# Two of four gate-logit rows summed on VectorE, w_gate turned in the prologue, and g split at the end of its own step

## The chip, the cores and the metric

The kernel runs on one core of one Trainium2 chip. Its time is the device time of one execution in microseconds (us). Of the kernel before there are three timed runs, told by their median, and one profiled execution. PE is TensorE, DVE is VectorE, ACT is ScalarE, POOL is GpSimd, and SP is SyncE, which here only issues transfers.

## The reference

Three parts follow one another: attention between 4096 tokens and 256 state rows (8 batches, 8 heads of 64), a layer g(h) = h - tanh(h) between two matrices, and a mixture of 8 experts that takes the best expert of each of 4608 rows.

```python
xread = softmax(scale * x @ state.T) @ state      # per batch and head
sread = softmax(scale * state @ x.T) @ x
x = concat(xread, sread).reshape(4608, 512)
h = x @ w_in                                      # 512 -> 2048
y = (h - tanh(h)) @ w_out                         # 2048 -> 512
logits = y @ w_gate                               # 512 -> 8
e = argmax(logits)
gate = softmax(logits)[e]
out[row] = gate * (relu(y @ w1[e]) @ w2[e])       # 512 -> 1024 -> 512
```

## The kernel before

The large products are taken in three parts: each operand is split into a high part that is exact in the fast matmul format and a low rest, and hi*hi, hi*lo and lo*hi are added up in PSUM. w_in and w_out come as 64-bit numbers, and three DVE operations (L186, L188, L191) with one of ACT turn a piece of 128 x 512 into float32: its decoding, `dec_bits`.

The work has three stages, one after the other:

- The prologue (up to about 130 us) does the attention scores, and multiplies the state with w_in, so that later h comes straight from the attention's probabilities. Its loop loads x in units (`xc`), three of them ahead; a list `later` holds stores, which SP issues at the head of each turn (`flush`, L451).
- The group stage (to about 779 us) runs 9 groups of rows. Groups 0 to 7 hold the 512 tokens of a batch as 4 rows of 128 each ("row" here is one such block of 128 tokens), group 8 holds the 256 state rows. Each group has 16 steps, one for each 128 of the 2048 columns of h. Step i does on PE `mm1(i)` (L828, six matmuls into `hp`), then `mm2(i-2)` (L858, twelve matmuls, three for each of the 4 rows, that add to the PSUM tiles y0 to y3). Between them lies the polynomial for g: ACT squares hp twice (L207, L208), DVE multiplies twice (L210, L211) into `gs`, `g_split` writes the high part `gh` (ACT, L847) and the rest `gl` (DVE, L160), and `g_check` (ACT, L840) records whether hp left the range of the polynomial. `hp` has two PSUM buffers, `gs` two, `gh` and `gl` three.
- The expert stage (to the end) takes blocks of 128 rows of one expert each. The change doesn't touch it.

In the group stage the order on PE, ACT, DVE and SP is that of the code, and each engine works in order. Four lists (`between`, `beside`, `after`, `moves`) say what else goes into which step, and where in it: `between` after mm1 on PE, `beside` after `g_split`, `after` behind `g_check`, `moves` last (transfers). While group 0 runs, w_out is decoded and split in every step; in groups 1 to 7 w_in is decoded again for group 8 in two or three steps of each (0 and 8, in groups 1 and 2 also 4), and a step later POOL takes the rest of that split. The operands of mm1 are split in steps 1, 2, 5, 6, 9, 10, 13 and 14 (`swl`), and in 10 and 12 (`atl`).

When a group is done, its rows are finished beside the next group's steps. In step 1, y0 to y3 are copied to `ys` in SBUF (three by ACT, one by DVE). Then each row r goes, two steps apart, through five operations: PE turns it with four transposes (`turn`, L263, end of step 2 + 2r), DVE copies the result (`turned`, L271, step 3 + 2r), PE multiplies it with w_gate in `parts` (L277, eight instructions, step 5 + 2r), ACT copies the partial sums (L283), and PE adds them up in `total` (L286, two instructions, step 6 + 2r). In step 12, when all four rows have their logits, DVE picks the expert (`choose`); `count` and `place` find each token's place in that expert's list.

## Time and profile before

| | |
|---|---|
| median of 3 runs | 1282.85 us (1280.61 to 1283.53) |
| profiled execution | 1281.19 us, span of its trace 1279.5 us |
| PE busy | 1229.9 us (96%) |
| DVE busy | 885.7 us (69%) |
| ACT busy | 858.0 us (67%) |
| POOL busy | 249.7 us (20%) |
| PE's share of the chain that ended last | 83% (L858 28%, L1426 16%, L1453 15%, L828 14%) |

Busy time counts an instruction from its start to its end; neighbours on one engine overlap, so what an instruction costs in a row of its kind is read from the starts, not from its length: twelve matmuls that each last 0.4 us start 0.23 us apart. A wait is the idle time before an instruction, put down to what ended it. The chain of waits goes back from the last instruction to what released each one.

### The profile page before, as it was taken

The numbers are of one execution on the slowest core, as the hardware profiler recorded it, in microseconds if no ns is written. First come the engines' busy times: TensorE is split into PE (matmuls) and PEld (weight loads), VectorE is DVE, ScalarE is ACT, GpSimd is POOL, SyncE is SP. The second block draws the span as 40 slices with busy tenths as digits, with TensorE's granted clock in tenths as the row PEclk, the third lists the DMA queues.
The fourth block names the chain that finished last, engine by engine and source line by source line (L and its number), as shares of the span: only waits on it lengthen the run. The fifth ranks groups of instructions, "written<-read, shape, count | busy, mean of one in ns | idle before, by whom it ended". The sixth has DMA issues, their size and how long they took to land.

```text
span 1279.5 us, 22682 instructions
## 1 busy us (share of the span) xinstructions
PE 1229.9 (96%) x6759; PEld 974.8 (76%) x6759; DVE 885.7 (69%) x1531; ACT 858.0 (67%) x1587; POOL 249.7 (20%) x299
## 2 busy tenths in 40 slices
PE   6989798999999999999999999999999999999995
PEld 4555576777777878778787888788888888888884
DVE  6999899677666766576666557567667677675663
ACT  7988687667676767667676674566666657565562
POOL 3333222011010101001010122322223322221100
PEclk8999899999999999999999999999999999999998
DMA  7999652413232222312222471744587867744241
GB/s 259 330 317 292 217 146 81 148 59 124 83 99 71 77 73 61 112 57 96 83 95 66 122 270 43 247 173 157 202 315 268 303 238 283 262 144 182 95 161 68
DMA packets 85777, 207.23 MB, mean 162 GB/s; under 512 B 9794, under 2 KB 26181, under 8 KB 83858
## 3 DMA queue, kind: packets, MB, share of 16 engines
q1 hardware_dynamic: 71186, 161.28, 37.8%
q0 software_dynamic: 14464, 44.40, 9.8%
q8 instruction: 62, 1.02, 0.3%
q14 instruction: 65, 0.53, 0.2%
HBM read 314.90 MB, written 74.51 MB: 304 GB/s over the span
## 4 chain that ended last, share of the span: by engine, by line
PE 83%; DVE 8%; DMA 4%; ACT 2%; issue 1%; SPq 0%; POOL 0%; DVEq 0%; POOLq 0%; ACTq 0%
PE y L858 28%; PE h L1426 16%; PE o L1453 15%; PE hp L828 14%; PE pt_h L1441 2%; DMA xc<-in_x_dram 2%; PE px L1264 1%; PE pt_y L263 1%; DVE dec_m L188 1%; DVE dec_m L191 1%; DMA atf<-probs_t 1%; DMA words<-in_moe_w_out_dram 1%; PE lg L277 1%; PE h_lead L1024 1%; DVE gl L160 1%
## 5 line engine op out<-in xcount | busy, mean ns | idle before, releaser
L858 PE MATMUL y<-w1t,gh 128*128 128x512 f32 x544 | 223.6, 411 | 2.2 <-ACT gh L847 2.2
L858 PE MATMUL y<-w1t,gl 128*128 128x512 f32 x544 | 218.3, 401 | 7.7 <-DVE gl L160 7.7
L210 DVE SCALAR_TENSOR_TENSOR gs<-gs,gu 128x512 f32<-128x512 f32 (+1 forms) x144 | 95.3, 662 | 179.2 <-ACT gs L208 167.6
L858 PE MATMUL y<-w,gh 128*128 128x512 f32 x544 | 215.7, 397 | 0.0
L1453 PE MATMUL o<-w2t,w 128*128 (+1 forms) x888 | 212.5, 395 | 0.8 <-DVE w2t L1370 0.8
L1426 PE MATMUL h<-w1t,w 128*128 (+1 forms) x888 | 212.2, 394 | 0.0
L1370 DVE TENSOR_TENSOR w2t<-w2raw,w2t 128x1024 f32 (+1 forms) x140 | 171.3, 1226 | 39.0 <-ACT w2t L1369 30.0
L1453 PEld LDWEIGHTS o<-w2t,w 128*128 128x128 f32 x888 | 163.9, 188 | 34.8 <-issue 1.2
L1426 PEld LDWEIGHTS h<-w1t,w 128*128 128x128 f32 x888 | 163.9, 188 | 33.7 <-issue 0.4
L207 ACT ACTIVATE gu<-hp 128x512 f32<-128x512 f32 (+1 forms) x144 | 82.4, 573 | 158.2 <-PE hp L828 157.8
L1369 ACT CAST w2t<-w2raw 128x1024 f32 (+1 forms) x140 | 147.1, 1053 | 17.0 <-DMA w2raw<-in_moe_w_dram 6.6
L858 PEld LDWEIGHTS y<-w1t,gl 128*128 128x128 f32 x544 | 103.3, 190 | 38.2 <-DVE gl L160 13.8
L828 PE MATMUL hp<-ath,swh 128*128 128x512 f32 (+1 forms) x320 | 122.5, 383 | 4.5 <-ACT ath L367 2.9
L858 PEld LDWEIGHTS y<-w1t,gh 128*128 128x128 f32 x544 | 103.0, 189 | 29.7 <-issue 6.4
L828 PE MATMUL hp<-atl,swh 128*128 128x512 f32 (+1 forms) x320 | 119.5, 373 | 0.9 <-DVE atl L368 0.9
L858 PEld LDWEIGHTS y<-w,gh 128*128 128x128 f32 x544 | 103.6, 190 | 21.8
L828 PE MATMUL hp<-ath,swl 128*128 128x512 f32 (+1 forms) x320 | 118.5, 370 | 0.0
L1432 ACT ACTIVATE hs<-h 128x512 f32<-128x512 f32 x74 | 43.8, 598 | 107.0 <-PE h L1426 102.8
L208 ACT ACTIVATE gs<-gu,b 128x512 f32<-128x512 f32 (+1 forms) x144 | 101.0, 701 | 7.1 <-DVE gl L160 1.9
L840 ACT ACTIVATE gu<-gu,nlim 128x512 f32<-128x512 f32 (+1 forms) x144 | 100.4, 697 | 6.4 <-DVE gs L210 5.0
L211 DVE SCALAR_TENSOR_TENSOR gs<-gs,hp 128x512 f32<-128x512 f32 (+1 forms) x144 | 94.6, 657 | 4.9
L160 DVE TENSOR_TENSOR gl<-gs,gh 128x512 fp32r<-128x512 f32 (+1 forms) x133 | 97.4, 733 | 0.0
(257 smaller groups left out, 1849.5 us busy)
## 6 DMA issues: line engine op xcount, KB each, us to landing
w1t<-w_parts SPq DMA_DIRECT2D x35, 4096.0 KB
w2raw<-in_moe_w_dram SPq DMA_DIRECT2D x140, 512.0 KB
w_parts<-w POOLq DMA_DIRECT2D x48, 512.0 KB
mot<-in_moe_w_dram SPq DMA_DIRECT2D x72, 256.0 KB
state_w_in<-swst SPq DMA_DIRECT2D x32, 512.0 KB
swf<-state_w_in SPq DMA_DIRECT2D x64, 256.0 KB
words<-in_moe_w_in_dram SPq DMA_DIRECT2D x16, 512.0 KB
xc<-in_x_dram SPq DMA_DIRECT2D x16, 512.0 KB
```

The source lines that it names most:

```text
L160: return eng.tensor_tensor(lo, t, hi.bitcast(F32), op=ALU.subtract)
L207: nc.scalar.activation(u, hp, AF.Square)
L208: nc.scalar.activation(s1, u, AF.Square, bias=b1)
L210: nc.vector.scalar_tensor_tensor(s1, s1, QD, u, op0=ALU.add, op1=ALU.mult)
L211: nc.vector.scalar_tensor_tensor(s1, s1, QC2, hp, op0=ALU.mult, op1=ALU.mult)
L828: nc.tensor.matmul(hp, a[:, c, o : o + P], m[:, c, :], start=(n == 0), stop=(n == 3 * chunks - 1))
L840: nc.scalar.activation(u, u, AF.Relu, bias=nlim, accum_out=over[:, n : n + 1])
L858: mm = nc.tensor.matmul(y, g, w[f], start=(f == 0 and n == 0), stop=(f == NF - 1 and n == 2))
L1369: hi = nc.scalar.copy(to[0](i * CH), t)
L1370: lo = nc.vector.tensor_tensor(to[1](SLOT + i * CH), t, to[1](i * CH).bitcast(F32), op=ALU.subtract)
L1426: mm = nc.tensor.matmul(h, a[:, k, :], part(w1t, o1, lo_ * SLOT + k * F2 + half * NX), start=(n == 0), stop=(n == 11),)
L1453: mm = nc.tensor.matmul(o, a[:, k, :], part(w2t, o2, lo_ * SLOT + k * DM), start=(n == 0), stop=(n == 23))
```

## The change

There are three parts.

- **Sums on DVE.** For groups 0 to 6, rows 0 and 1 no longer go through `turn`, `turned`, `parts`, copy and `total`. For each of these rows and each of the 8 experts DVE multiplies the row of 512 with that expert's column of w_gate, laid out along the free dimension and repeated on all partitions (`wgb`), and adds up the product in the same instruction (`sums`, one scalar_tensor_tensor with `accum_out`; the product itself goes to `junk`). That is 16 instructions of 128 x 512 per group, put into steps 2 to 11: two each in steps 2, 3, 5, 7, 8 and 10, one in 4, 6, 9 and 11. Rows 2 and 3 keep their path and their steps. `choose` first copies their logits from PSUM next to the sums. Group 7 and group 8 stay as they were.
- **w_gate turned.** In the prologue PE turns w_gate (four transposes of 128 x 32, `turn_gate`, behind the first `attn_x`), DVE copies the result of 8 x 512, and SP stores it to DRAM at the next `flush`. In steps 2 to 9 SP loads each of its 8 rows back onto all 128 partitions, 256 KB each. `wgb` lies in a half of `w1t` that held four of the eight `pairs`, the ring through which the w_in parts go; the ring now has four. PSUM for the logits is taken when it is first used, no longer when a group's finish begins.
- **g_split.** `gh` and `gl` of step i were made in step i + 1, right behind the two multiplications for that step. They are now made at the end of step i, behind `beside` and `g_check` (in step 0 ahead of `beside`).

```diff
--- before.py
+++ after.py
@@ -1,3 +1,4 @@
+import functools
 import itertools
 from contextlib import ExitStack
 
@@ -42,6 +43,7 @@
         "w1": nc.dram_tensor("w1_parts", (E * P, 2, DM // P * F2), F32).ap(),
         "wi": nc.dram_tensor("w_in_parts", (FF // (2 * P), P, 2, 2, DM), F32).ap(),
         "at": nc.dram_tensor("probs_t", (B, P, 2, S), F32).ap(),
+        "wg": nc.dram_tensor("w_gate_t", (E, DM), F32).ap(),
         "sw": nc.dram_tensor("state_w_in", (FF // NX, B // 4, H, 4, NS, NX), F32).ap(),
     }
     args = (tc, x, state, w_in.bitcast(I32), w_out.bitcast(I32), w_gate, w1, w2, out, scratch)
@@ -83,8 +85,8 @@
 
     NSURE = NBLK + (E - 1) * 3 // 4
     scale = 1.0 / float(D) ** 0.5
-    yd, lists, w1s, wis, atd, swd = (
-        scratch[k] for k in ("y", "list", "w1", "wi", "at", "sw")
+    yd, lists, w1s, wis, atd, swd, wgd = (
+        scratch[k] for k in ("y", "list", "w1", "wi", "at", "sw", "wg")
     )
 
     const = ctx.enter_context(tc.tile_pool(name="const", bufs=1))
@@ -228,13 +230,26 @@
             self.pool, self.psp, self.b = pool, psp, b
             self.nr = R if b < B else NSR
             self.pt, self.yT = {}, {}
-            lg = psp.tile([P, 3 * R * E + P], F32, tag="lg", name="lg")
-            self.lg = lg[:, 0 : 3 * self.nr * E].rearrange("p (i r e) -> p i r e", i=3, e=E)
-            self.lgt = lg[:, 3 * R * E :]
             self.ys = pool.tile([P, self.nr, DM], F32, tag="ys", name="ys", bufs=1)
+
+            self.summed = 0 if b > B - 2 else self.nr // 2
+            if self.summed:
+                self.logit = pool.tile([P, self.nr, E], F32, tag="logit", name="logit", bufs=2)
             self.lgs = pool.tile([P, self.nr, E], F32, tag="lgs", name="lgs", bufs=2)
             self.entry = pool.tile([P, self.nr, 2], F32, tag="entry", name="entry", bufs=2)
             nc.gpsimd.tensor_copy(self.entry[:, :, 0], ridf[:, b * R : b * R + self.nr])
+
+        @functools.cached_property
+        def bank(self):
+            return self.psp.tile([P, 3 * R * E + P], F32, tag="lg", name="lg")
+
+        @property
+        def lg(self):
+            return self.bank[:, 0 : 3 * self.nr * E].rearrange("p (i r e) -> p i r e", i=3, e=E)
+
+        @property
+        def lgt(self):
+            return self.bank[:, 3 * R * E :]
 
         def take(self, r, y):
             if r < self.nr - 1:
@@ -285,6 +300,13 @@
         def total(self, r):
             nc.tensor.matmul(self.lg[:, 0, r], self.lgs2, sel, start=True, stop=True)
 
+        def sums(self, r, e):
+            junk = self.pool.tile([P, DM], F32, tag="junk", name="junk", bufs=1)
+            nc.vector.scalar_tensor_tensor(
+                junk, self.ys[:, r], 1.0, wgb[:, e], op0=ALU.mult, op1=ALU.mult,
+                accum_out=self.logit[:, r, e : e + 1],
+            )
+
         def logits(self, r):
             yT = self.yT.pop(r)
             for k in range(NPR):
@@ -297,7 +319,9 @@
 
         def choose(self):
             nr, lgs = self.nr, self.lgs
-            lg = self.lg[:, 0]
+            lg = self.logit if self.summed else self.lg[:, 0]
+            if 0 < self.summed < nr:
+                nc.vector.tensor_copy(lg[:, self.summed :], self.lg[:, 0, self.summed :])
             mx = self.small("rmx")
             nc.vector.tensor_reduce(mx, lg, axis=AX.X, op=ALU.max)
             mxb = mx.unsqueeze(2).to_broadcast([P, nr, E])
@@ -491,6 +515,14 @@
             c = slice(2 * k, 2 * k + 2)
             nc.scalar.copy(sth[:, c], st[:, c])
             rest(nc.vector, stl[:, c], st[:, c], sth[:, c])
+
+        def turn_gate():
+            pt = ps_m.tile([P, NPR, P], F32, tag="m", name="pt_gate")
+            for k in range(NPR):
+                nc.tensor.transpose(pt[0:QR, k, :], wg[:, k], ident)
+            t = tmp("e2", (P, NX))
+            nc.vector.tensor_copy(t[0:E], pt[0:E].rearrange("p k m -> p (k m)"))
+            later.append((wgd, t[0:E]))
 
         win = {}
         wdec = Decoder(pa, 3)
@@ -687,6 +719,7 @@
             for o, j in ((0, 0), (0, 4), (1, 0), (1, 4), (1, 8)):
                 turn_state(o, j)
             attn_x(0)
+            turn_gate()
             for i in piece(1):
                 wdec.absolute(i)
                 wdec.bits(i)
@@ -790,6 +823,9 @@
         ps_m = pe.enter_context(tc.tile_pool(name="ps_m", bufs=1, space=PSUM, reuse_waits="tile"))
 
         pairs = w1t[:, 0].rearrange("p h n -> p (h n)").rearrange("p (i h n) -> p i h n", h=2, n=NX)
+        pairs = pairs[:, 0 : pairs.shape[1] // 2]
+
+        wgb = w1t[:, 0, 1, 0 : E * DM].bitcast(F32).rearrange("p (e d) -> p e d", e=E)
         turns = itertools.count()
 
         def pair():
@@ -898,6 +934,12 @@
             put(moves, i + 1, store_win, f)
         for g in range(NF // 2):
             put(moves, B * NF + 2 * g - 3, load_win, g)
+
+        def gate_load(e):
+            nc.sync.dma_start(wgb[:, e], wgd[e : e + 1].to_broadcast([P, DM]))
+
+        for e in range(E):
+            put(moves, 2 + e, gate_load, e)
         def finish(b, i):
             fn = Finish(fin, ps_m, b)
             for r in range(fn.nr):
@@ -905,7 +947,10 @@
             if b == B:
                 return fn
             put(moves, i + 1, fn.store)
-            for r in range(fn.nr):
+            all_ = [(r, e) for r in range(fn.summed) for e in range(E)]
+            for n, a in enumerate(all_):
+                put(beside, i + 1 + n * 10 // len(all_), fn.sums, *a)
+            for n, r in enumerate(range(fn.summed, fn.nr)):
                 j = i + 2 * r
                 put(after, j + 1, fn.turn, r)
                 put(beside, j + 2, fn.turned, r)
@@ -1085,11 +1130,13 @@
                     mm2(b, f)
                     if f == NF - 1:
                         fn = finish(b, i)
-                if 1 <= i <= N:
-                    g_split(*seq[i - 1])
+                if i == 0:
+                    g_split(*seq[i])
                 run(beside, i)
                 if i < N:
                     g_check(*seq[i])
+                if 0 < i < N:
+                    g_split(*seq[i])
                 run(after, i)
                 run(moves, i)
 
```

DVE in steps 7 and 8 of group 1, from the two multiplications of step 7 on; `gs_3238` and `gs_3278` are gs of these steps. Before:

```order
L210 SCALAR_TENSOR_TENSOR gs_3238<-gs_3238,gu 128x512
L211 SCALAR_TENSOR_TENSOR gs_3238<-gs_3238,hp 128x512
L160 TENSOR_TENSOR gl<-gs_3192,gh 128x512
L271 COPY yT<-pt_y 128x512
L210 SCALAR_TENSOR_TENSOR gs_3278<-gs_3278,gu 128x512
L211 SCALAR_TENSOR_TENSOR gs_3278<-gs_3278,hp 128x512
L160 TENSOR_TENSOR gl<-gs_3238,gh 128x512
L186 TENSOR_SCALAR dec_l<-words 128x512
L188 SCALAR_TENSOR_TENSOR dec_m<-dec_m,dec_l 128x512
L191 SCALAR_TENSOR_TENSOR dec_m<-words,dec_m 128x512
```

And now, where the two gs are `gs_3249` and `gs_3290`:

```order
L212 SCALAR_TENSOR_TENSOR gs_3249<-gs_3249,gu 128x512
L213 SCALAR_TENSOR_TENSOR gs_3249<-gs_3249,hp 128x512
L305 SCALAR_TENSOR_TENSOR junk,logit<-ys,w1t 128x512 x2
L286 COPY yT<-pt_y 128x512
L162 TENSOR_TENSOR gl<-gs_3249,gh 128x512
L212 SCALAR_TENSOR_TENSOR gs_3290<-gs_3290,gu 128x512
L213 SCALAR_TENSOR_TENSOR gs_3290<-gs_3290,hp 128x512
L188 TENSOR_SCALAR dec_l<-words 128x512
L190 SCALAR_TENSOR_TENSOR dec_m<-dec_m,dec_l 128x512
L193 SCALAR_TENSOR_TENSOR dec_m<-words,dec_m 128x512
L305 SCALAR_TENSOR_TENSOR junk,logit<-ys,w1t 128x512 x2
L162 TENSOR_TENSOR gl<-gs_3290,gh 128x512
```

The gl that stands behind the two multiplications of a step was that of the step before; now each step ends with its own, behind the decoding and the two sums.

ACT in steps 2 and 3 of group 1, where `gs_2977` was the g of step 1 and `gs_3023` that of step 2. Before:

```order
L207 ACTIVATE gu<-hp 128x512
L208 ACTIVATE gs_3023<-gu,b_70 128x512
L847 CAST gh<-gs_2977 128x512
L367 CAST swh<-swf 128x512
L840 ACTIVATE gu,over<-gu,nlim 128x512
L207 ACTIVATE gu<-hp 128x512
L208 ACTIVATE gs_3070<-gu,b_70 128x512
L847 CAST gh<-gs_3023 128x512
L840 ACTIVATE gu,over<-gu,nlim 128x512
```

And now, where `gs_3043` and `gs_3089` are the g of steps 2 and 3:

```order
L209 ACTIVATE gu<-hp 128x512
L210 ACTIVATE gs_3043<-gu,b_70 128x512
L391 CAST swh<-swf 128x512
L876 ACTIVATE gu,over<-gu,nlim 128x512
L883 CAST gh<-gs_3043 128x512
L209 ACTIVATE gu<-hp 128x512
L210 ACTIVATE gs_3089<-gu,b_70 128x512
L876 ACTIVATE gu,over<-gu,nlim 128x512
L883 CAST gh<-gs_3089 128x512
```

gh moves from behind the two squares, where its gs had been done for most of a step, to the end of the step, where the same step's gs has just been made.

SP at the start of the program, from the first piece of w_in on (`words`). Before:

```order
L175 DMA words<-in_moe_w_in_dram 128x1024
L537 DMA xc<-in_x_dram 128x4x256
L175 DMA words<-in_moe_w_in_dram 128x1024
L537 DMA xc<-in_x_dram 128x4x256
L175 DMA words<-in_moe_w_in_dram 128x1024
L537 DMA xc<-in_x_dram 128x4x256
L175 DMA words<-in_moe_w_in_dram 128x1024
L751 DMA expert_lists<-unlisted 128x560
```

And now:

```order
L177 DMA words<-in_moe_w_in_dram 128x1024
L569 DMA xc<-in_x_dram 128x4x256
L177 DMA words<-in_moe_w_in_dram 128x1024
L569 DMA xc<-in_x_dram 128x4x256
L177 DMA words<-in_moe_w_in_dram 128x1024
L477 DMA w_gate_t<-e_246 8x512
L569 DMA xc<-in_x_dram 128x4x256
L177 DMA words<-in_moe_w_in_dram 128x1024
L784 DMA expert_lists<-unlisted 128x560
```

The third load of x, which followed the third piece of w_in at once, now stands behind the store of the turned w_gate.

## Rows read from the trace of the kernel before

**Rows 1.** Windows: span, busy us by engine (instructions), TensorE clock, DMA share, GB/s.

```profile
145.00:200.00 55.00, 50.23 (x194) 37.52 (x194) 52.74 (x74) 44.52 (x87) 15.88 (x12) 0.95 0.52 152
555.00:628.00 73.00, 73.00 (x358) 57.80 (x358) 48.24 (x90) 51.26 (x103) 7.09 (x7) 1.00 0.25 80
```

**Rows 2.** Timeline, PE, groups 5 and 6, mm1's first matmul: start us, us, operation.

```profile
553.48 0.40 PE L828 MATMUL hp<-ath,swh 128*128 128x512 f32 x1
...
558.23 0.40 PE L828 MATMUL hp<-ath,swh 128*128 128x512 f32 x1
...
562.65 0.40 PE L828 MATMUL hp<-ath,swh 128*128 128x512 f32 x1
...
566.84 0.40 PE L828 MATMUL hp<-ath,swh 128*128 128x512 f32 x1
...
584.05 0.40 PE L828 MATMUL hp<-ath,swh 128*128 128x512 f32 x1
...
588.60 0.48 PE L828 MATMUL hp<-ath,swh 128*128 128x512 f32 x1
...
592.88 0.39 PE L828 MATMUL hp<-ath,swh 128*128 128x512 f32 x1
```

**Rows 3.** Timeline, two steps of group 1, PE and DVE (in brackets: idle before).

```profile
240.21 0.40 PE L828 MATMUL hp<-ath,swh 128*128 128x512 f32 x1
...
242.29 0.40 PE L858 MATMUL y<-w1t,gl 128*128 128x512 f32 x1
...
243.19 0.69 DVE L210 SCALAR_TENSOR_TENSOR gs<-gs,gu 128x512 f32<-128x512 f32 x1 [0.44 <-ACT gs L208]
...
243.92 0.69 DVE L211 SCALAR_TENSOR_TENSOR gs<-gs,hp 128x512 f32<-128x512 f32 x1
...
244.52 0.68 DVE L160 TENSOR_TENSOR gl<-gs,gh 128x512 fp32r<-128x512 f32 x1
```

**Rows 4.** Timeline, one step of group 0, DVE and POOL.

```profile
176.47 0.68 DVE L210 SCALAR_TENSOR_TENSOR gs<-gs,gu 128x512 f32<-128x512 f32 x1
...
177.19 0.69 DVE L211 SCALAR_TENSOR_TENSOR gs<-gs,hp 128x512 f32<-128x512 f32 x1
...
177.29 1.30 POOL L160 TENSOR_TENSOR w<-dec_m,w1t 128x512 fp32r<-128x512 f32 x1 [3.14 <-ACT w1t L197]
...
177.79 1.34 DVE L160 TENSOR_TENSOR gl<-gs,gh 128x512 fp32r<-128x512 f32 x1
...
179.06 0.41 DVE L186 TENSOR_SCALAR dec_l<-words 128x512 int32<-128x512 int32 x1
...
180.91 0.68 DVE L210 SCALAR_TENSOR_TENSOR gs<-gs,gu 128x512 f32<-128x512 f32 x1
```

**Rows 5.** Timeline, PE, two of its waits (in brackets: length, releaser).

```profile
195.20 0.63 PE L858 MATMUL y<-w1t,gl 128*128 128x512 f32 x1 [2.28 <-DVE gl L160]
...
776.72 0.50 PE L858 MATMUL y<-w1t,gl 128*128 128x512 f32 x1 [0.63 <-DVE gl L160]
```

**Rows 6.** Groups by line: count | busy us, mean ns | idle before.

```profile
L840 ACT ACTIVATION_READ_ACCUMULATOR gu<-gu,nlim 128x1 f32 x144 | 27.1, 188 | 0.0
...
L271 DVE COPY yT<-pt_y 128x512 f32<-128x512 f32 x29 | 19.7, 681 | 0.3 <-PE pt_y L263 0.3
```

**Rows 7.** Timeline, the prologue's first steps, SP's queue, PE and DVE.

```profile
4.80 0.62 SPq L537 DMA_DIRECT2D xc<-in_x_dram  x1
...
9.41 1.06 PE L548 MATMUL pt_x<-ident,xc 128*128 128x128 f32 x8 [1.25 <-DMA xc<-in_x_dram]
...
11.76 0.69 DVE L188 SCALAR_TENSOR_TENSOR dec_m<-dec_m,dec_l 128x512 int32<-128x512 int32 x1 [1.55 <-ACT dec_m L181]
...
18.52 0.66 PE L548 MATMUL pt_x<-ident,xc 128*128 128x128 f32 x4
```

**Rows 8.** Chain of waits, two of its pieces: start us, us, what.

```profile
44.61 6.27 DMA xc<-in_x_dram
...
172.17 11.50 DMA words<-in_moe_w_out_dram
```

## The prediction, made before the changed kernel ran

> **What bounds the kernel now.** I read first the windows, to see which engine is full in which stretch, then the timeline of PE, step by step, and last who waits for whom. In groups 1 to 7 PE is full: 73.00 of 73 us, while DVE is busy 48.24 and no other engine is near full [rows 1]. There every PE instruction taken out shortens the step by its issue time, as long as no other engine becomes late. Group 0 is different: in its window PE is busy 50.23 of 55 us and DVE 52.74 [rows 1], because the decoding of w_out stands in every step. DVE's operations follow each other without a gap: from one first multiplication to the next 4.44 us [rows 4], where a plain step of PE takes 4.19 (562.65 to 566.84) [rows 2]. So in group 0 work taken from PE would be worth nothing, and the order on DVE decides. No PE instruction is removed there anyway.
>
> **The sums: what PE loses.** The price of one row's path comes from the starts of mm1. A plain step is 4.19 us. The step with `parts` (553.48 to 558.23) is 4.75, so parts cost 0.56. The step with `total` (558.23 to 562.65) is 4.42: 0.23. The step that ends with a row's transposes (584.05 to 588.60) is 4.55: 0.36, and the next (588.60 to 592.88) is 4.28, 0.09 more for the change back to long matmuls [rows 2]. One row costs 0.56 + 0.23 + 0.36 + 0.09 = 1.24 us of PE. Two rows in each of seven groups: 14 x 1.24 = 17.4 us. All of it lies in steps where PE is the bound. This is the main term, -17.4.
>
> **The sums: what DVE gets.** Sixteen instructions per group that read two SBUF tensors of 128 x 512. No row shows one with an accumulator on DVE. Nearest are its multiplications of the same shape: start to start 0.73 us where the second needs the first (243.19 to 243.92) and 0.60 where it doesn't (243.92 to 244.52) [rows 3]. ACT's accumulator shows a second instruction of 188 ns behind each of its own [rows 6]. So a sum costs at least 0.60, and at most two passes of 0.69 and such a read-out, 1.57. I take 0.8, near the multiplication, since nothing in a row shows a two-SBUF multiplication of DVE at half rate.
>
> Does it fit? In steps 2 to 11 DVE has, without the sums, 10 x (0.73 + 0.60 + 0.60) = 19.3 for g, six splits (3.6) and two copies of turned rows (1.2) at 0.60, one decoding at 1.85 (179.06 to 180.91) and one collision with POOL at 0.67 (gl takes 1.27, 177.79 to 179.06, in place of 0.60) [rows 3, 4]: 26.6 us. PE needs for these ten steps 41.9 and for what rows 2 and 3 still bring (two turns 0.90, two parts 1.12, one total 0.23) 2.25, so 44.15. That leaves 17.5 us for 16 sums, or 1.09 each, before DVE falls behind. At 0.8 they take 12.8.
>
> A single step can still be late. With the change gl(i) is the last operation of step i. Its first multiplication starts 2.98 us behind the start of mm1(i) (240.21 to 243.19) and the two and gl itself take 0.73 + 0.60 + 0.68, so gl(i) is there at 5.0 + W, W being what `beside` has on DVE. PE needs it in mm2(i), two steps on: 8.38 + 1.85 = 10.2 us behind mm1(i) (242.29 less 240.21, less the 0.23 of the total in that step) [rows 2, 3]. The slack is 5.2 - W. The fullest step is 8, decoding and two sums, W = 3.45; behind it, steps 9 and 10 start with about 1 us of arrears and W of 2.7 to 2.8. So PE's gl comes in time by 1 to 2 us, and hp too, whose buffer is freed already by the second multiplication. Queued behind the sums on DVE are gl and the next step's multiplications; behind gh on ACT, the next step's squares. In step 1 ACT also copies three y tiles, which makes the squares of step 2 late as before. I put down +1 us for waits in all seven groups (0 to +5). The small copy in `choose` lies in step 12, which has no sums: nothing.
>
> A rule of the Trainium skill speaks against this price: the page "Vector Engine (DVE) Microarchitecture Reference", section "Points that are easy to get wrong", says that a scalar_tensor_tensor with two non-bf16 sources in SBUF runs at half throughput, since both read ports are taken and none is left for the accumulator. The trace has the two-source fp32 multiplication without an accumulator at 0.69 us, not double, and shows none with one. By that rule the sum would come out as in the third rival below.
>
> **g_split at the end of its own step.** In groups 1 to 7 PE hardly waits for gl, so nothing is to be had there. In group 0 gl(i) moves ahead of the next step's two multiplications, of 0.73 and 0.60, and of a collision of 0.67: PE can run mm2(i) up to 2.0 us earlier, and its wait of 2.28 us for gl [rows 5] is of this kind. That lead is kept when DVE stops being the bound, at the start of group 1. I take -2 (0 to -4). DVE's own work doesn't change. What is new is that gh, and so ACT's next squares, hang on the same step's second multiplication; from there gh and two squares take about 2 us on ACT, while DVE has the decoding and gl to do, 1.85 + 0.60, so DVE doesn't idle. POOL's subtraction now starts earlier against DVE's order and will block another operation. A blocked operation waits until POOL's 1.30 us are over [rows 4]: between 0.67, as now, and 1.3 per step. I take +0.5 for the group (0 to +10, 16 steps at 0.63 more). At the end of the stage the wait of 0.63 us in mm2's last step [rows 5] goes: -0.6 (0 to -0.6), and what is late next there is the copy of y.
>
> **w_gate in the prologue.** PE's four transposes stand behind the first x unit, which starts at 9.41 and lasts 1.06; DVE's copy of their result costs 0.68, like the copy of a turned row [rows 6, 7]. So it runs from about 10.95 to 11.6, and the first decoding behind it starts at about 12.1 and not at 11.76. DVE's work is the chain of most of the prologue: +0.4 (0 to +1). SP's third x load was issued at 4.80; now it waits behind the store for that copy, until about 12.1. A load of x took 6.27 us when the DMA engines were full [rows 8], so it would land by 18.4, and PE's transposes of that unit began at 18.52 [rows 7]. It just fits; if not, it costs tenths, which the bound of +1 holds.
>
> The eight loads of `wgb` bring 2 MB into group 0's steps 2 to 9. SP issues them behind the same step's load of w_out. One such load there took 11.50 us and was on the chain [rows 8], while the DMA share was 0.52 [rows 1], so there is room but a piece can be late: +1 (0 to +4).
>
> **Sum.** -17.4 + 1 - 2 + 0.5 - 0.6 + 0.4 + 1 = -17.1. I round to -17. The profiled execution took 1281.19 us, 1.69 outside its span of 1279.5; less 17 that is 1264.2. The median of the runs is 1.66 above the profiled one, so I expect a median of 1266.
>
> **Rivals.** (a) Group 0 gets longer: POOL's collisions cost the full 1.3 in every step (+10), and the w_out loads slip. For it: DVE is full there, and ACT now hangs on it. Against it: the second multiplication ran its 0.69 us beside POOL [rows 4], so one operation per step is blocked, as before. Time: 1266 + 10 = 1276.
>
> (b) Group 0 gets shorter than I say. DVE's step there is 4.44 with a blocked gl of 1.27 in it; were POOL's subtraction, which now starts earlier against DVE's order, to fall beside the decoding, 0.67 would go and DVE would need 3.77, so that PE's 4.19 is the step [rows 2, 4]: 16 x 0.25 = 4, and with POOL's +0.5 gone 4.5. For it: a decoding of 1.85 is long enough to hold 1.30. Against it: it has the same order in each step now, and gl is still the two-SBUF operation behind it. Time: 1266 - 5 = 1261.
>
> (c) A sum costs two passes, 1.38 us. Sixteen take 22.1 where 17.5 fit; 4.6 behind, less the slack of step 11, 5.2 - 1.38 = 3.8: 0.8 us wait per group, and 2.5 more in groups 1 and 2, whose third decoding (1.85 + 0.67) lies in these steps. 7 x 0.8 + 5 = 10.6 lost: 1266 + 10.6 - 1 (the waits counted already) = 1276.
>
> (d) The other side: two passes and a read-out, 1.57 us, make DVE the bound in steps 2 to 11 of groups 1 to 7. Sixteen take 25.1, 7.6 too much; less 3.6 of slack PE waits 4.0 us per group, and with the third decodings 28 + 5 = 33, against 17.4 saved: 1283 + 33 - 17 - 1 = 1298. At s us a sum PE waits 17 x s - 22.7 + 0.7 per group (16 sums, less 17.5 and the slack of 5.2 - s; the third decodings add 5 over seven groups). That passes 0 at 1.3 us, where the gain begins to shrink, and the 2.48 saved per group at 1.44, from where the kernel is slower. For it: no row shows the operation. Against it: all DVE multiplications of this shape last 0.69.
>
> **How the numbers follow.** My forecast 0.60, (a) 0.12, (b) 0.11, (c) 0.08, (d) 0.09. The forecast's own range is 1262 to 1271, from the bounds of its terms taken half. To leave out no more than 2 in 10 I go on to (b) below and to (a) and (c) above: 1260 to 1277. What this kernel's measurement can tell from no change is about 0.2%, 2.6 us. Faster are the forecast, (a), (b) and (c), whose times are all more than 6 us below, less 0.03 for a sum between (c) and (d): 0.88. Slower is (d): 0.09. Within 0.2%: 0.03.
>
> **What would show it.** Right: mm1 starts 4.19 us apart in steps 3, 4 and 5 of groups 1 to 7, where step 3 was 4.28; a group takes 2.48 us less; PE full there; a sum of 0.6 to 0.9 us; DVE busy about 60 of 70 us per group (48.24 less two copies, 16 sums more); PE's waits for gl in group 0 shorter; mm1(0) not more than 1 us later. Wrong: waits of PE for gl or of mm1 for the second multiplication in steps 8 to 12 (the sums are dearer, or the arrears larger); a group 0 longer by several us, with more than one long DVE operation per step or with DVE waiting for `words`; sums of 1.2 us or more.

## The result and the profile after

The changed kernel takes 1260.27 us (median of 4 runs, 1258.44 to 1263.43) against 1281.73 for the kernel before in the same comparison: a ratio of 0.9836, 95% interval 0.9818 to 0.9854, or 21 us less. The forecast was 1266 in a range of 1260 to 1277. The two profiled executions differ by less than the medians: 1281.19 and 1263.43 us, spans 1279.5 and 1261.7, so 17.8 us of span; the profiled execution of the changed kernel is the slowest of its four.

Where the 17.8 us went is read from the first matmul of mm1 in each group's step 0, and from the ends of the spans (us). In group 0 alone the mark is the fourth of mm1's six matmuls, since PE takes the first three ahead of the prologue's last product (`px`), at 130.41 us before and 132.40 after; "group 0" below always counts from that fourth one, and so does "step 0 starts".

| stretch | before | after | difference |
|---|---|---|---|
| prologue, up to the fourth matmul of step 0 | 133.74 | 135.04 | +1.30 |
| group 0 | 79.06 | 76.05 | -3.01 |
| group 1 | 73.24 | 70.16 | -3.08 |
| groups 2 to 7, each | 72.40 | 69.96 | -2.44 |
| group 8, steps 0 to 14 | 51.91 | 53.25 | +1.33 |
| from there to the end | 507.08 | 507.49 | +0.41 |

With six groups of -2.44 the sum is -17.7. First the windows of [rows 1] in the changed kernel (columns: span, busy us by engine with instructions, clock, DMA share, GB/s):

```profile
145.00:200.00 55.00, 48.97 (x196) 36.71 (x195) 51.54 (x77) 46.86 (x90) 19.17 (x12) 0.97 0.66 191
555.00:628.00 73.00, 73.00 (x335) 58.47 (x334) 59.51 (x130) 53.60 (x106) 7.31 (x7) 1.00 0.26 80
```

In the second PE is still full, with 335 matmuls where there were 358: the same step work passes in less time. DVE has gone from 48.24 to 59.51 us. The timeline of PE shows the steps in group 6 of the changed kernel (the stretch that answers [rows 2]); of each step only the first matmul of mm1 is listed here:

```profile
561.06 0.40 PE L864 MATMUL hp<-ath,swh 128*128 128x512 f32 x1
565.25 0.40 PE L864 MATMUL hp<-ath,swh 128*128 128x512 f32 x1
569.45 0.40 PE L864 MATMUL hp<-ath,swh 128*128 128x512 f32 x1
573.64 0.40 PE L864 MATMUL hp<-ath,swh 128*128 128x512 f32 x1
577.83 0.40 PE L864 MATMUL hp<-ath,swh 128*128 128x512 f32 x1
582.03 0.40 PE L864 MATMUL hp<-ath,swh 128*128 128x512 f32 x1
586.22 0.40 PE L864 MATMUL hp<-ath,swh 128*128 128x512 f32 x1
590.77 0.48 PE L864 MATMUL hp<-ath,swh 128*128 128x512 f32 x1
595.05 0.39 PE L864 MATMUL hp<-ath,swh 128*128 128x512 f32 x1
```

Steps 0 to 5 are 4.19 or 4.20 us apart, where steps 2 and 3 were 4.55 and 4.28 [rows 2]; the first turn now stands in step 6 (586.22 to 590.77, 4.55). What it costs DVE is in the groups by line (count, busy us, mean ns, idle before):

```profile
L305 DVE SCALAR_TENSOR_TENSOR junk<-ys,w1t 128x512 f32<-128x512 f32 x112 | 76.9, 687 | 1.5
...
L305 DVE DVE_READ_ACCUMULATOR junk<-ys,w1t 128x1 f32 x112 | 9.1, 82 | 0.0
```

A sum is one pass of 0.69 us and a read-out of 0.08. The timeline of DVE in a step of group 7 with two sums shows how they stand together:

```profile
644.48 0.68 DVE L392 TENSOR_TENSOR swl<-swf,swh 128x512 fp32r<-128x512 f32 x1
645.08 0.69 DVE L305 SCALAR_TENSOR_TENSOR junk<-ys,w1t 128x512 f32<-128x512 f32 x1
645.69 0.08 DVE L305 DVE_READ_ACCUMULATOR junk<-ys,w1t 128x1 f32 x1
645.81 0.69 DVE L305 SCALAR_TENSOR_TENSOR junk<-ys,w1t 128x512 f32<-128x512 f32 x1
646.43 0.08 DVE L305 DVE_READ_ACCUMULATOR junk<-ys,w1t 128x1 f32 x1
646.43 0.69 DVE L162 TENSOR_TENSOR gl<-gs,gh 128x512 fp32r<-128x512 f32 x1
647.03 0.68 DVE L212 SCALAR_TENSOR_TENSOR gs<-gs,gu 128x512 f32<-128x512 f32 x1
```

From one sum to the next 0.73 us, and to gl 0.62. DVE comes out of this step without a gap (647.03), that is in arrears, but PE does not wait for it: between 215 and 700 us the trace shows no wait of PE at all.

Group 0 is the stretch that the forecast had least right. A step like that in [rows 4], now with gl at its end (timeline of DVE and POOL):

```profile
159.22 0.68 DVE L162 TENSOR_TENSOR gl<-gs,gh 128x512 fp32r<-128x512 f32 x1
...
159.82 0.68 DVE L212 SCALAR_TENSOR_TENSOR gs<-gs,gu 128x512 f32<-128x512 f32 x1
...
160.04 1.63 POOL L162 TENSOR_TENSOR w<-dec_m,w1t 128x512 fp32r<-128x512 f32 x1 [2.54 <-ACT w1t L199]
160.54 0.69 DVE L213 SCALAR_TENSOR_TENSOR gs<-gs,hp 128x512 f32<-128x512 f32 x1
161.15 0.81 DVE L188 TENSOR_SCALAR dec_l<-words 128x512 int32<-128x512 int32 x1
162.06 0.69 DVE L190 SCALAR_TENSOR_TENSOR dec_m<-dec_m,dec_l 128x512 int32<-128x512 int32 x1
162.79 0.69 DVE L193 SCALAR_TENSOR_TENSOR dec_m<-words,dec_m 128x512 int32<-128x512 int32 x1
163.40 0.68 DVE L162 TENSOR_TENSOR gl<-gs,gh 128x512 fp32r<-128x512 f32 x1
164.00 0.68 DVE L212 SCALAR_TENSOR_TENSOR gs<-gs,gu 128x512 f32<-128x512 f32 x1
```

gl runs in 0.68, no longer 1.34. POOL's subtraction starts one multiplication earlier against DVE's order, inside L212, takes 1.63 in place of 1.30, and the operation that stretches is the decoding's shift (L188), 0.81 in place of 0.41. The step of DVE is 164.00 - 159.82 = 4.18 us where it was 4.44, so PE's own 4.19 is the step now. Two longer waits of PE stand late in this group; a load and a collision of another operation with POOL lie behind them (timeline of PE, ACT, DVE and POOL, in brackets what each waited for):

```profile
185.10 0.43 DVE L188 TENSOR_SCALAR dec_l<-words 128x512 int32<-128x512 int32 x1 [0.84 <-DMA words<-in_moe_w_out_dram]
185.16 0.68 ACT L183 ACTIVATE dec_m<-words 128x512 f32<-128x512 f32 x1 [3.12 <-DMA words<-in_moe_w_out_dram]
...
187.11 0.50 PE L894 MATMUL y<-w1t,gh 128*128 128x512 f32 x1 [1.05 <-ACT gh L883]
...
189.93 1.58 POOL L162 TENSOR_TENSOR w<-dec_m,w1t 128x512 fp32r<-128x512 f32 x1 [6.22 <-ACT w1t L199]
...
190.27 1.79 DVE L392 TENSOR_TENSOR atl<-atf,ath 128x512 fp32r<-128x512 f32 x1
...
194.57 0.50 PE L894 MATMUL y<-w1t,gl 128*128 128x512 f32 x1 [2.14 <-DVE gl L162]
```

ACT stands 3.12 us for a load of w_out, and gh is queued behind it, so PE waits 1.05 us. This is the load whose 11.50 us are in the chain of [rows 8]. The next step has a split more (`atl`), and POOL holds it up: 1.79 us where the same split takes 0.68 elsewhere. Its gl comes late by both, and the wait of 2.28 in [rows 5] is still 2.14. The wait of 0.63 at the end of the stage [rows 5] is gone, but the time from the last mm1 to the end is no shorter (the table's last line).

### The profile page after: what moved, and what is told of

Read it like the earlier page. It is cut to its first block, busy times and chain, and to the rows that moved or that the text cites. A ratio compares the mean times of both kernels' runs of the same rounds, so it can differ in the third digit from the quotient of the medians.

```text
span 1261.7 us, 22408 instructions
## 1 busy us (share of the span) xinstructions
PE 1214.7 (96%) x6567; PEld 965.8 (77%) x6567; DVE 942.3 (75%) x1749; ACT 863.9 (68%) x1573; POOL 253.2 (20%) x299
## 5 line engine op out<-in xcount | busy, mean ns | idle before, releaser
L894 PE MATMUL y<-w1t,gh 128*128 128x512 f32 x544 | 220.5, 405 | 1.5 <-ACT gh L883 1.0
L212 DVE SCALAR_TENSOR_TENSOR gs<-gs,gu 128x512 f32<-128x512 f32 (+1 forms) x144 | 95.1, 660 | 84.2 <-ACT gs L210 84.2
L162 DVE TENSOR_TENSOR gl<-gs,gh 128x512 fp32r<-128x512 f32 (+1 forms) x133 | 90.5, 680 | 14.9 <-ACT gh L883 13.4
```

Source lines behind the costliest of these rows:

```text
L162: return eng.tensor_tensor(lo, t, hi.bitcast(F32), op=ALU.subtract)
L212: nc.vector.scalar_tensor_tensor(s1, s1, QD, u, op0=ALU.add, op1=ALU.mult)
L894: mm = nc.tensor.matmul(y, g, w[f], start=(f == 0 and n == 0), stop=(f == NF - 1 and n == 2))
```

## The experiments

All times below are medians of fresh runs, each with the kernel before on the same chip; the ratios and 95% intervals are to that. Times of groups and steps come from one profiled execution of each kernel.

**Only the sums, without the moved split.** The edit to the changed kernel:

```
-                if i == 0:
-                    g_split(*seq[i])
+                if 1 <= i <= N:
+                    g_split(*seq[i - 1])
                 run(beside, i)
                 if i < N:
                     g_check(*seq[i])
-                if 0 < i < N:
-                    g_split(*seq[i])
```

> The changed kernel, but gh and gl are made in the next step again, behind its two multiplications, as in the kernel before. Theory 1 (the terms of the sum stand side by side): groups 1 to 7 stay at 69.95 us, and only what was put down for the move comes back, 2 us in group 0 and 0.6 at the end of the stage: about 1263 against the changed kernel's 1260. Theory 2 (the move is what lets the sums fit): with gl behind the next step's multiplications it is there about 4.2 + 5.0 = 9.2 us after mm1 of its step, 1.0 us before PE needs it, and DVE's arrears in the steps with two sums (1.93 + 1.5 + a split 0.6 or a decoding 1.85, against 4.19) are more than that: PE waits 1 to 3 us per group for gl, groups of 71 to 73 us, 1267 to 1280.

Measured: 1265.59 us, ratio 0.9863 (0.9844 to 0.9882), 5.3 us above the changed kernel. Groups 2 to 7 take 69.94, so theory 2 falls: the sums fit in either order. Theory 1 holds for them, but it had 2.6 us for the move where the medians say 5.3 (the two ratios say 3.5). Group 0 takes 79.26, as before the change and 3.2 more than in the changed kernel. Its DVE has the old collision:

```profile
162.90 1.30 POOL L162 TENSOR_TENSOR w<-dec_m,w1t 128x512 fp32r<-128x512 f32 x1 [3.18 <-ACT w1t L199]
163.37 1.38 DVE L162 TENSOR_TENSOR gl<-gs,gh 128x512 fp32r<-128x512 f32 x1
```

**Only the moved split.** The same edit the other way round, made to the kernel before:

```
-                if 1 <= i <= N:
-                    g_split(*seq[i - 1])
+                if i == 0:
+                    g_split(*seq[i])
                 run(beside, i)
                 if i < N:
                     g_check(*seq[i])
+                if 0 < i < N:
+                    g_split(*seq[i])
```

> The kernel before with one edit: gh and gl at the end of their own step (step 0 excepted). No sums, no w_gate in the prologue. Theory 1: groups 1 to 7 stay at 72.40 us; group 0 shorter by about 2 us and the wait of 0.63 us at the end of the stage gone: 1279 against 1281.7. Theory 2 (DVE is full in group 0 and its work is the same): nothing, 1281 to 1282. Theory 3 (POOL's subtraction now falls beside another operation of DVE, blocked for 0.40 in place of 0.67 us, as the trace of the changed kernel shows it): 16 x 0.25 more, group 0 shorter by 4 to 5 us, 1277.

Measured: 1276.78 us against 1282.47, ratio 0.9950 (0.9932 to 0.9969). 5.7 us less, theory 3. Groups 2 to 7 stay at 72.40, group 0 falls from 79.06 to 74.00, its plain steps from 4.45 to 4.19. In its steps the shift is held up in place of gl, and by less (timeline of DVE and POOL):

```profile
158.44 1.62 POOL L160 TENSOR_TENSOR w<-dec_m,w1t 128x512 fp32r<-128x512 f32 x1 [2.54 <-ACT w1t L197]
159.55 0.80 DVE L186 TENSOR_SCALAR dec_l<-words 128x512 int32<-128x512 int32 x1
```

**POOL's subtraction later, split not moved.** To tell the collision from the place of gl, in the kernel before:

```
-            put(beside, f, dec_split, 0, f)
+            put(after, f, dec_split, 0, f)
```

> The kernel before with one edit in group 0: ACT's cast of the decoded w_out row, which releases POOL's subtraction, stands behind ACT's check and no longer ahead of it, about 1.5 us later; DVE's and PE's orders and the place of gh and gl are as before. POOL's 1.30 us then start at about 178.6 in the step of rows 4, when gl has ended, and fall beside the decoding. Theory 1 (what POOL's subtraction falls beside sets DVE's step, and so the gain of the moved split): steps of group 0 fall from 4.43 to about 4.2, group 0 shorter by about 4 us, 1278.5 against 1282.5. Theory 2 (gl ahead of the next step's multiplications is what counts): steps stay at 4.43, 1282 to 1283.

Measured: 1286.06 us against 1283.91, ratio 1.0014 (0.9998 to 1.0029). Neither theory gave this: steps went to 4.70. But the rows say why, and in favour of theory 1's cause, if not of its number (timeline of DVE and POOL):

```profile
163.10 0.69 DVE L160 TENSOR_TENSOR gl<-gs,gh 128x512 fp32r<-128x512 f32 x1
163.70 0.42 DVE L186 TENSOR_SCALAR dec_l<-words 128x512 int32<-128x512 int32 x1
163.89 1.39 POOL L160 TENSOR_TENSOR w<-dec_m,w1t 128x512 fp32r<-128x512 f32 x1 [3.32 <-ACT w1t L197]
164.23 1.60 DVE L188 SCALAR_TENSOR_TENSOR dec_m<-dec_m,dec_l 128x512 int32<-128x512 int32 x1
165.86 0.69 DVE L191 SCALAR_TENSOR_TENSOR dec_m<-words,dec_m 128x512 int32<-128x512 int32 x1
```

gl escaped, the next operation with two SBUF inputs did not, and lost 0.91 (1.60 for 0.69). So DVE's step is 3.77, its length without collision, and what the collision takes: 3.77 + 0.67 = 4.44 in the kernel before, 3.77 + 0.40 = 4.17 in the changed one, 3.77 + 0.91 = 4.68 here (4.70 measured). The smallest loss is the one in which the whole of the second multiplication falls beside POOL's subtraction; it reads PSUM and ran its 0.69 in every case.

**w_gate turned and loaded, but no row summed.** In the changed kernel:

```
-            self.summed = 0 if b > B - 2 else self.nr // 2
+            self.summed = 0
```

> The changed kernel with no row summed: w_gate is turned in the prologue, stored, and loaded in group 0, and gh and gl stand at the end of their step, but all four rows go through PE as before. It differs from the kernel in which only the split was moved (1276.8 us) by the w_gate work alone. Theory 1: +0.4 in the prologue and +2 in group 0, where the loads stand between those of w_out (group 0 took 76.0 us with them and 74.0 without, from mm1 of step 0 to that of step 16): 1279; groups 1 to 7 at 72.40. Theory 2: the loads find room, and the 2 us were the scatter of single runs: 1276.5 to 1277.5.

Measured: 1276.63 us, ratio 0.9962 (0.9947 to 0.9977), against 1276.78 and 0.9950 with the split alone. By the medians this is theory 2. But the intervals overlap, and by the two ratios w_gate would cost 1.5 us: these runs show no cost, and can't rule out one of that size. Its groups 2 to 7 take 72.40, as before the change: without the sums, the halved ring and the later use of PSUM change nothing there. Its profile has group 0 at 75.31, and step 0 starts at 133.15. In the ten profiles of kernels with the moved split group 0 takes 74.0 to 76.1, and step 0 starts at 131.8 to 136.5 us with w_gate in the prologue and at 133.7 to 137.8 without, so the changed kernel's +1.30 there lies within the scatter of single profiles.

**The loads of w_gate's rows seven steps later.**

```
-            put(moves, 2 + e, gate_load, e)
+            put(moves, 9 + e, gate_load, e)
```

> The changed kernel with the eight loads of w_gate's rows issued in steps 9 to 16 in place of 2 to 9, so that most of them come behind the last loads of w_out. Theory 1 (the loads delay those of w_out): group 0 goes from 76.0 to about 74 us, 1258.3 against 1260.3. Theory 2 (the waits for w_out have another cause, the loads of state and probabilities queued ahead of them): group 0 stays at 75.5 to 76, 1260 to 1261.

Measured: 1259.31 us, ratio 0.9816 (0.9801 to 0.9832), not told apart from the changed kernel's 1260.27. Group 0 takes 75.59, and ACT's wait is as long without any such load ahead of it, so theory 2:

```profile
181.64 0.68 ACT L183 ACTIVATE dec_m<-words 128x512 f32<-128x512 f32 x1 [3.26 <-DMA words<-in_moe_w_out_dram]
```

**Every sum twice.**

```
             nc.vector.scalar_tensor_tensor(
                 junk, self.ys[:, r], 1.0, wgb[:, e], op0=ALU.mult, op1=ALU.mult,
                 accum_out=self.logit[:, r, e : e + 1],
             )
+            (the same four lines again)
```

> The changed kernel with every sum issued twice, 32 in place of 16 per group of 0 to 6; the second writes the same values. A sum took 0.69 us and its read-out 0.08 in the changed kernel, some 0.76 from start to start, so this is a sum of 1.52. Theory 1 (the room is that of steps 2 to 11, 17 x s - 22.0 per group): PE waits 3.8 us per group, 27 in all, 1287, slower than the kernel before; the waits are for gl or of mm1 for the second multiplication in steps 8 to 12. Theory 2 (the room is that of the whole group: DVE is busy some 57 of 70 us, so 12.2 more just fit): arrears are worked off later at no cost, groups of 70 to 71 us, 1260 to 1267.

Measured: 1292.85 us, ratio 1.0075 (1.0052 to 1.0098): slower than the kernel before, which is theory 1's direction, and by more than its 1287. Groups 3 to 7 take 73.72, 3.76 above the changed kernel; groups 1 and 2, with a third decoding, 78.25 and 76.68, so 8.1 and 6.7 above it. Some waits of group 3 (timeline of PE):

```profile
404.22 0.66 PE L278 MATMUL pt_y<-ident,ys 128*128 128x128 f32 x4 [1.33 <-DVE yT L286]
...
412.39 0.51 PE L898 MATMUL y<-w1t,gl 128*128 128x512 f32 x1 [0.71 <-DVE gl L162]
...
422.81 0.50 PE L898 MATMUL y<-w1t,gl 128*128 128x512 f32 x1 [0.98 <-DVE gl L162]
```

gl is late as expected. The first wait was not named by any theory: the second row's transposes wait for DVE's copy of the first one's, which is queued behind the sums. Of PE's 25.7 us of waits in groups 1 to 7, 10.3 are of this kind, one in each group.

**Three rows summed.**

```
-            self.summed = 0 if b > B - 2 else self.nr // 2
+            self.summed = 0 if b > B - 2 else self.nr - 1
```

> The changed kernel with three rows in place of two summed on DVE in groups 0 to 6, 24 sums spread over steps 1 to 10, and one row through PE. Theory 1: seven more row paths of 1.24 us go, -8.7; 24 sums take 24 x 0.76 = 18.2 where about 17 fit before arrears and some 4 of slack stand behind them, so PE hardly waits: groups of 68.7 us, 1252. Theory 2: with 2.4 sums a step DVE falls behind by more than its slack and PE waits what it gained: 1258 to 1262.

Measured: 1256.08 us, ratio 0.9795 (0.9773 to 0.9817). Groups 3 to 7 come to 68.71, 1.25 less. Groups 1 and 2 rise to 71.68 and 70.50 (from 70.16 and 69.96), and with them about half of the expected 8.7 is missing. In both, PE waits behind a third decoding (timeline of DVE, POOL and PE in group 2):

```profile
325.92 1.30 POOL L162 TENSOR_TENSOR w1t<-dec_m,w1t 128x512 fp32r<-128x512 f32 x1 [16.70 <-issue]
...
325.98 1.79 DVE L162 TENSOR_TENSOR gl<-gs,gh 128x512 fp32r<-128x512 f32 x1
327.69 0.68 DVE L212 SCALAR_TENSOR_TENSOR gs<-gs,gu 128x512 f32<-128x512 f32 x1
...
327.82 0.51 PE L894 MATMUL y<-w1t,gl 128*128 128x512 f32 x1 [0.55 <-DVE gl L162]
```

**Three rows, the third decodings moved.** To the kernel with three rows:

```
-        spare = [b * NF + f for b in range(B - 1) for f in ((0, 4, 8) if b < 2 else (0, 8))]
+        spare = [b * NF + f for b in range(B - 1) for f in ((0, 8, 13) if b < 2 else (0, 8))]
```

> The kernel with three rows summed, and the third decoding of w_in in groups 1 and 2 moved from their step 4 to their step 13, behind the sums. Theory 1 (these decodings, 1.85 us of DVE and a gl blocked by POOL for 1.1, are why groups 1 and 2 took 71.67 and 70.50 us and not 68.71): both groups come to about 68.8, 1256.1 - 4 = 1252. Theory 2 (the start of the stage is the cause, something else than the decoding): they stay above 70, 1255 to 1257.

Measured: 1252.72 us (1251.45 to 1254.29), ratio 0.9763 (0.9749 to 0.9776), theory 1: groups 1 and 2 take 68.93 and 69.43, together 3.8 less; group 3 takes 69.50 where it took 68.71, which was not expected. This beats both kernels, the one before by 30 us.

**All four rows summed.** The sums are spread over 13 steps, 2 to 14, with the choice in step 15:

```
-            self.summed = 0 if b > B - 2 else self.nr // 2
+            self.summed = 0 if b > B - 2 else self.nr
...
-                put(beside, i + 1 + n * 10 // len(all_), fn.sums, *a)
+                put(beside, i + 1 + n * (10 if fn.summed < fn.nr else 13) // len(all_), fn.sums, *a)
...
-            i = j + 5
+            i = j + 5 if fn.summed < fn.nr else i + 14
```

The later choice of group 6 pushes the last three of the 16 pieces of the lead expert's weights behind the stage's last step, and they are left out; group 8 and the total are therefore no measure, and only groups 1 to 7 are read.

> The changed kernel with all four rows of groups 0 to 6 summed on DVE, 32 sums spread over steps 1 to 13 and the choice of experts in step 14; no transposes or logits of these groups on PE. PE needs 72.40 - 4 x 1.24 = 67.4 us a group. DVE was busy some 46.5 in the kernel before; less four copies of 0.68 and with 32 sums of 0.73 start to start it needs 67.2. Theory 1 (DVE as the bound): the two are level, each blocked gl of 1.8 us and each decoding shows, groups of 68.5 to 70 us, 1255 to 1263, no better than three rows (1256.1). Theory 2 (spread over more steps they fit): groups of 67.4 us, 1256.1 - 7 x 1.3 = 1247.

Measured: 1264.03 us, with groups 3 to 7 at 68.8, against 67.4 for PE alone and 68.71 with three rows. Theory 1. One window (columns as above):

```profile
555.00:628.00 73.00, 72.22 (x311) 57.86 (x310) 70.62 (x163) 52.86 (x104) 7.74 (x7) 1.00 0.28 83
```

PE stands idle for 0.78 us here, each time for gl, while DVE is at 70.62 of 73: the fourth row has no room.

**The loads of w_out a step earlier.** To the best kernel:

```
-            put(moves, f - 3, dec_load, 0, f)
+            if f >= 3:
+                put(moves, max(f - 4, 0), dec_load, 0, f)
```

> The kernel with three rows summed and the third decodings moved (1252.7 us), and the loads of w_out's words for steps 4 to 15 of group 0 issued one step (4.2 us) earlier, in the step in which their buffer comes free. Theory 1 (these loads come late because they are issued late: in step 11 ACT stood 3.0 us for one, and the steps there took 5.8 and 7.5 us in place of 4.2): the stall goes or shrinks by 4 us, 1248.5. Theory 2 (the DMA queues are full there, and an earlier issue only lengthens the time to landing): group 0 as long as before, 1252 to 1253.

Measured: 1253.86 us, ratio 0.9760 (0.9738 to 0.9783), not told apart from the kernel without it (0.9763). Group 0 takes 74.52 in place of 75.44. The load comes in time, but ACT now stands for the next ones in the queue (timeline of ACT):

```profile
183.58 0.62 ACT L391 CAST swh<-swf 128x512 fp32r<-128x512 f32 x1 [1.46 <-DMA swf<-state_w_in]
188.85 0.62 ACT L391 CAST ath<-atf 128x512 fp32r<-128x512 f32 x1 [0.40 <-DMA atf<-probs_t]
190.20 0.68 ACT L183 ACTIVATE dec_m<-words 128x512 f32<-128x512 f32 x1 [0.20 <-DMA words<-in_moe_w_out_dram]
```

**And the lead expert's pieces a step earlier.** On top of that:

```
-                    put(moves, o - 2, lead_load, p)
+                    put(moves, o - 3, lead_load, p)
```

> As the kernel with the words loaded a step earlier, and the pieces of the lead expert's weights in group 8 loaded a step earlier too. Theory 1 (group 8's steps of 4.0 to 5.3 us in place of 3.5 to 3.7, and its 57.4 us against the 56.1 of the kernel before, are ACT's wait for such a piece, 2.9 us in the changed kernel): 1 to 1.5 us less than without it, 1247 to 1251. Theory 2 (the DMA engines are full there, share 0.92): no difference.

Measured: 1254.82 us, ratio 0.9764 (0.9742 to 0.9787). No gain; group 8 takes 52.66 us, and 52.46 without the edit. The +1.33 of group 8 in the changed kernel can't be tied to the change either: with the split alone it took 52.63, with split and w_gate 51.97, and with POOL's subtraction later, which has no part of the change, 52.80.

## Why the prediction was right, and where it was not

The main mechanism was right, the rows that leave PE where PE is full. The total was less so: the result lies 0.3 us inside the stated range, and below the forecast's own 1262 to 1271.

**The rows, -17.4: right.** Seven groups gave 6 x 2.44 + 3.08 = 17.7, of which 0.6 belongs to group 1's start, which hung on group 0: with the sums but the old split group 1 took 70.77 in place of 70.16. The price of a row's path, 1.24 by differences between steps, came back as 1.22 a row (2.44 for two) and as 1.25 for the third (69.96 - 68.71).

**The sum's price, 0.8 taken, 0.73 measured: right, and with it the waits.** PE's +1 for waits was 0. The rivals (c) and (d) fell with the price. The rule of the Trainium skill that was weighed against it, in "Vector Engine (DVE) Microarchitecture Reference", section "Points that are easy to get wrong" (two non-bf16 SBUF sources at half throughput), does not hold for this operation: with an accumulator it took 0.687 us, where the plain multiplication takes 0.69 [rows 3]. Of the arithmetic of (d) the direction held: with every sum twice the kernel was slower. Its size did not, though 3.76 us a group looks like the 3.8 of 17 x s - 22 at 1.52 us a sum. That formula is a mean over seven groups with 0.7 in it for the third decodings; groups 3 to 7 have none, so for them it is 17 x s - 22.7, which gives 3.1, or 2.1 at the 2 x 0.73 that a doubled sum took. For groups 1 and 2 it gives 5.6 at most, and 8.1 and 6.7 were measured. The wait for the copy of a turned row was not in it.

**g_split at the end of its step, -2 and -0.6, and POOL's collisions, +0.5: the step that was mis-sized.** Together they stood for -2.1; measured, -5.7 alone and, by medians, -5.3 as the difference between the sums with and without it. The gain did not come from where the -2 saw it: the wait of 2.28 us that was to shrink is still 2.14, since it hangs on the load and on `atl`. Nor is the -0.6 to be seen in the time. What was missed is the size of the collision. The prediction said of the earlier subtraction that it would block another operation for 0.67 to 1.3 us. It blocks one for 0.40, and so DVE's step falls below PE's. This is rival (b), given 0.11, in its time of 1261, but not in its way: the decoding's shift doesn't hide POOL, it loses 0.40, and there are no 16 equal steps of 0.25. Steps 4 to 10 are 0.24 to 0.31 shorter each, 1.9 us together (32.92 to 31.07). Steps 2 to 15 together take 68.2 to 70.3 us in the ten profiles with the moved split, and 73.7 and 73.4 in the two with the split and POOL's start as they were; what the steps outside 4 to 10 add to this was not taken apart, and steps 11 and 12 alone scatter between 11.4 and 14.1.

The loss follows how much of POOL's span is left when the next operation comes up that POOL can block: 0.80 in the kernel before (178.59 less 177.79 [rows 4], 0.67 lost), 0.52 in the changed one (161.67 less 161.15, 0.40 lost), 1.05 with POOL later (165.28 less 164.23, 0.91 lost). It is 0.12 to 0.14 less than that each time. That some of POOL's span costs nothing was to be read from [rows 4], since the second multiplication ran beside POOL unharmed there: an earlier start lays more of POOL's span against it. The range held because (b) was in it, whose way was another: that much is luck.

The Trainium skill's "SBUF — State Buffer", section "Who interferes with whom", says that a DVE operation holds a port pair that POOL also needs if both its inputs are in SBUF or if it runs in a two-port mode, which copy, cast and tensor_scalar can, and that whoever is second waits for the first to end. The trace agrees on both sides: POOL started inside L212 and took 0.3 more, and the shift of one SBUF input, 0.41 alone, took 0.81 beside it.

**w_gate, +0.4 and +1: too small to be told.** With the split and w_gate the time is 0.2 us below that with the split alone by medians, and 1.5 above it by ratios. One reading behind the +0.4 was wrong: the third load of x did not just fit. It was issued at 13.18 us, not at about 12.1, and PE's transposes of that unit began at 21.22, where they had begun at 18.52 [rows 7] (timeline of SP's queue and PE, changed kernel):

```profile
13.18 0.39 SPq L569 DMA_DIRECT2D xc<-in_x_dram  x1
...
21.22 0.66 PE L580 MATMUL pt_x<-ident,xc 128*128 128x128 f32 x4
```

In the ten profiles with w_gate in the prologue the third unit begins 7.2 to 8.7 us behind the second, in the three without 6.2 to 6.4. By the fourth unit nothing is left of it: 16.4 to 18.5 us behind the second with w_gate, 16.7 to 17.8 without.

**The sum.** By medians the parts are -5.7 for the split and -16.5 for sums with w_gate (1276.78 to 1260.27): -22.2 against the whole of -21.5. The forecast's -17 came from -2.1 for the first and -15 for the second.

What stays open: why a load of w_out takes some 11 us to land late in group 0 (11.50 in [rows 8]), and what it costs. Steps 11 and 12 take 11.4 to 14.1 us together in every kernel, where two plain ones take 8.4, but the late `atl` is in this too. An issue one step earlier made this load come in time, with no gain in the whole, and the loads of w_gate's rows seven steps later changed nothing; other loads of the stretch were not moved.

## What to carry to other kernels

Price a piece of PE's work by differences between steps in a stretch where PE is full, and then count what the engine that takes it over has left in just the steps in question, its arrears and slack included; that sum told here the gain of two rows and that doubled sums turn it into a loss, though not how large a loss; of the third row's gain half came only when the third decodings were moved out of the way. When an edit moves one engine's instructions against another's, look at which operation stands beside a blocking neighbour before and after: a move that changes no work changed DVE's step by the difference of what was blocked (0.67, 0.40 or 0.91 us). Once one engine is full, a next gain can be had by moving what else stands in the same steps, as the third decodings here.

## What was not expected of the hardware

A POOL subtraction of 128 x 512 takes 1.30 us, or about 1.6 where it starts inside a DVE operation with two SBUF inputs, and what it costs DVE changes with where it starts: 0.67 us with gl behind it, 0.91 with an integer combination of two tensors, 0.40 where DVE's multiplication with a PSUM operand covers more of it, and 1.1 (gl or `atl` 1.79) where nothing does. A DVE sum with accumulator costs hardly more than the plain multiplication: 0.69 and 0.08 us, with the next operation starting 0.62 to 0.73 us after it.
